# Due times shifted by phase in an attention and gated-mix kernel

## The chip, the cores and the metric

One core of a Trainium2 chip runs the whole program. The metric is the device time of one execution in microseconds (us). The kernel before was timed in three runs; the median is 744.59 us (743.41 to 746.06).

## The reference

The inputs are q, k and v of 8 batches, 8 heads, 576 positions and 64 elements, a scalar tau, and the weights of a gated mix. All is float32.

```python
def _attn_ref(q, k, v, tau):
    scores = scale * np.matmul(q, k.transpose(0, 1, 3, 2))
    thresh = np.max(scores, axis=-1, keepdims=True) - tau
    scores = np.where(scores >= thresh, scores, -1000000000.0)
    scores = scores - np.max(scores, axis=-1, keepdims=True)
    attn = np.exp(scores)
    attn = attn / (np.sum(attn, axis=-1, keepdims=True) + 1e-09)
    return np.matmul(attn, v)

def _moe_ref(x, w_val, conv_w, w_out):      # x: heads side by side, 8 x 576 x 512
    xp = np.concatenate([np.zeros((B, K - 1, D)), x], axis=1)
    for k in range(K):                      # K = 5 taps
        gate_pre += conv_w[k] * xp[:, k:k + S, :]
    gate = 1.0 / (1.0 + np.exp(-gate_pre))
    return gate * (x @ w_val) @ w_out
```

The threshold lies tau below the largest score of a row, so the maximum is taken first, and the exponentials under the threshold are dropped.

## The kernel before

A *job* is a pair of heads of one batch; there are 32 jobs, four to a batch. Each job has nine *score tiles*: one of 64 query rows of both heads together ("both"), and eight of 128 query rows of one head, so 288 tiles in all, numbered k in program order. A tile goes through these steps, each one a planned operation:

- `Tile.multiply` (L519, matmul at L537) on TensorE: scores into one of two PSUM rooms `s`. Keys are split into a high and a low float32r part, so an ordinary tile takes four matmuls and a tile of both heads six.
- `largest` (L541) on VectorE takes the row maximum; `weigh` (L547) on ScalarE makes `e`, the exponentials, and the threshold; `keep` (L560, L570) on VectorE drops what lies under the threshold, sums the rows, writes `pp` (or `pl` for both heads) and gives the room `s` back.
- `Group.divided` (L585, L603 on GpSimd, or L599 when ScalarE is free first) divides by the sums. The first batch divides later, after the product with v.
- `Group.turn` (L647, L659) on TensorE transposes blocks of three 128-column pieces into one of two PSUM rooms `tp`; `copy` (L663, L670) on ScalarE moves them into `T`.
- `Half.attended` (L722) has two parts for each half of the queries of a job: `attend` (L733), 20 matmuls of T and v into one of two PSUM rooms `acc`, and `evacuate` (L744; L742 on VectorE in the first batch), which copies into `xT`.

Around them run `Job.prepare` (L329: loads, splits and scaling of the next job's q and k; `place` at L368 lays blocks of q on GpSimd) and `subtract` (L295, L302: the low parts of splits, on GpSimd, for k, q, x and the gated values). `convolve` (L812) makes the high part of x (`xh`, L818 on ScalarE), the first tap (`tap0`, L828 on GpSimd), four more taps (L835 on VectorE) and the gate (L843). In the first batch the taps are matmuls (L788).

`products` (L864) runs once a batch: 96 matmuls of w_val with x, in chains of 12 into one `acc` each, gated on VectorE (L909), split into gh (`high`, L925 on ScalarE) and gl (`subtract`); then 96 of w_out (L882), evacuated on ScalarE (L947) and stored. Products come strictly one after another. Six rooms each hold xh and xl, so the first products of a batch must be done before the third job of the next can store its parts.

In what order all this stands on each engine's queue is settled when the program is built. Every operation has a *due* rank, in units of tiles, and a planned cost. `carry_out` (L134) walks through planned time. On each engine it finds the earliest time at which some operation can begin, given its inputs, its rooms and the engine; among all that can begin by then it takes the smallest due. The engines work through the resulting queues in order, waiting on semaphores. Due decides only between operations that are ready together in the plan.

Ranks that bear on the change: scores k - 8, with k the tile's number; reduce and weigh k - 8; keep k - 8; a division k - 4; a turn k - 3 + 0.1 c0; attend k - 2; evacuation of xT k - 4 (k being the last tile of the group or half). Products have the tile count at the batch's end plus 4, and 0.17 more for each matmul. xh, tap0 and the taps stand near the tile count at the job's end.

Of the kernel before, what the change touches and what calls it, by code (L numbers as in the profile page):

```python
# [20 lines left out]
AHEAD = False  # L21
TH = "ACT"
DIVIDE = ("ACT",)
DUE = (8, 8, 8)
PACE_M = 0.17
EARLY = 3
LATE = 1
ON_PE = (0, 1, 2, 3)
WARM = 10
FILL = 6  # L30


@with_exitstack
def tile_thresholded_attention_gated_mix(
# [88 lines left out]
    def op(engine, due, cost, done, emit, after=(), takes=(), gives=(), other=()):  # L123

        ways = {w[0]: w[1:] for w in ((engine, cost, done, emit), *other)}
        o = Op(ways, due, after, takes, gives)
        if not o.waits:
            for e in ways:  # L130
                open_ops[e].append(o)
        return o
# [41 lines left out]
    r_acc = Rooms(None, 0, None, None, None)  # L174
# [30 lines left out]
    def keep_busy(n):  # L205
        for _ in range(n):
            nc.tensor.matmul(r_tp.free[0][1], some[:, 0:P], some, start=True, stop=True)  # L207
# [21 lines left out]
    def from_f64(words, a, m, f, due, wide, after=(), takes=()):  # L229


        i32 = lambda t: t.bitcast(I32)
        hi, lo = lambda: words()[..., 1], lambda: words().bitcast(U16)[..., 1]
        least = 2.0**-15 * 1.125
        c1, c2 = (0.21, 0.345) if wide else (0.1, 0.12)
        square = op(
            "ACT", due, 0.34, 0.5, lambda: nc.scalar.square(f, hi().bitcast(F32)), after
        )
        last = op("DVEp", due, c1, c1 + 0.1, lambda: nc.vector.tensor_scalar(
            i32(m), hi(), 3, 0x3FFFFFFF, op0=ALU.logical_shift_left, op1=ALU.bitwise_and), after)  # L240
        last = op("DVEp", due, c2, c2 + 0.1, lambda: nc.vector.scalar_tensor_tensor(
            i32(a()), hi(), -(1 << 30), i32(m), op0=ALU.bitwise_and, op1=ALU.bitwise_or),
            [last], takes)
        last = op("DVEp", due, c2, c2 + 0.1, lambda: nc.vector.scalar_tensor_tensor(  # L244
            a(), f.bitcast(F32), least * least, a(), op0=ALU.is_ge, op1=ALU.mult), [last, square])
        last = op("DVEp", due, c1, c1 + 0.1, lambda: nc.vector.tensor_scalar(
            i32(m), i32(a()), -(1 << 23), None, op0=ALU.bitwise_and), [last])
        last = op("DVEp", due, c2, c2 + 0.1, lambda: nc.vector.scalar_tensor_tensor(
            f, lo(), 2.0**-36, m, op0=ALU.mult, op1=ALU.mult), [last])
        add = op("POOL", due, 0.71 if wide else 0.2, 0.8 if wide else 0.3,  # L250
                 lambda: nc.gpsimd.tensor_add(a(), a(), f.bitcast(F32)), [last])
        return last, add
# [218 lines left out]
    class Tile:  # L471
        def __init__(self, k, t, h, qc, grp):
# [16 lines left out]
            elif t.last == (h, qc):  # L489
                gives = [(r_Q, lambda: t.Q), (r_KH, lambda: t.KH), (r_KL, lambda: t.KL)]  # L490
            cost = 1.0 if t.i == 0 else 0.80 if both else 0.54
            self.scores = op(
                "PE", k - DUE[0], cost, cost + 0.26, self.multiply, after, [r_s], gives,
            )
            largest = op("DVE", k - DUE[1], 0.67, 0.84, self.largest, [self.scores], [r_nm])
            if TH == "ACT":
                after = [op("ACT", k - DUE[1], 0.83, 1.0, self.weigh, [largest], [r_e])]
            else:
                after = [
                    op("ACT", k - DUE[1], 0.64, 0.78, self.weigh, [largest], [r_e]),  # L500
                    op("DVE", k - 9, 0.13, 0.13, self.level, [largest]),
# [7 lines left out]
            else:  # L509
                room.append(r_sums)  # L510
            grp.kept = op(
                "DVE", k - DUE[2], 0.74, 0.96, self.keep, after, room,
                [(Scores(k), lambda: self.s), (r_e, lambda: self.e), (r_nm, lambda: self.nm)],
# [5 lines left out]
        def multiply(self):  # L519
# [18 lines left out]
            if self.k == EARLY - 1:  # L538
                keep_busy(FILL)

# [145 lines left out]
    class Half:  # L686
# [35 lines left out]
        def attended(self, k):  # L722
            t, j = self.t, self.j
            w, x0 = W[j], PAD + HALVES[j].start

            def attend():
                acc = self.acc = r_acc.take()
                T = self.T[:, :, 0:w]
                for c in (NKC, *range(NKC)):
                    for h, hs in enumerate(HEADS):  # L730
                        c0 = (2 * c + h) * D
                        chunk = 2 * NKC if c == NKC else h * NKC + c
                        nc.tensor.matmul(  # L733
                            acc[hs, :w], t.v[:, c0 : c0 + D], T[:, chunk, :],
                            start=c == NKC, stop=c == NKC - 1, skip_group_check=True,
                        )

            def evacuate():
                if j == 0:
                    t.xT = r_xT.take()  # L740
                if t.b < LATE:
                    nc.vector.tensor_mul(t.xT[:, x0 : x0 + w], self.acc[:, :w], self.R[:, W[0] - w :])  # L742
                else:
                    nc.scalar.copy(t.xT[:, x0 : x0 + w], self.acc[:, :w])  # L744

            cost = 5 * w / 600 + 0.1
            gives = [(r_T, lambda: self.T)]
            if j == 1:
                gives.append((r_v, lambda: t.v))
            made = op("PE", k - 2, cost, cost + 0.2, attend, [t.got_v, *self.copies], [r_acc], gives)  # L750
            cost = 0.31 if j == 0 else 0.255
            after = [made] if j == 0 else [made, t.got_x]
            gives = [(r_acc, lambda: self.acc)]
            if t.b < LATE:
                cost += 0.085
                after.append(self.inverses(k))
                gives.append((r_R, lambda: self.R))
            t.got_x = op("DVE" if t.b < LATE else "ACT", k - 4, cost, cost + 0.2, evacuate, after,
                         [r_xT] if j == 0 else [], gives)
            t.got_half.append(t.got_x)  # L760

# [311 lines left out]
```

## Time and profile before

| | |
|---|---|
| median of three runs | 744.59 us |
| profiled execution, its own time | 745.84 us |
| its span, first to last instruction | 744.1 us |
| TensorE busy | 728.5 us, 98% |
| ScalarE busy | 632.6 us, 85% |
| VectorE busy | 602.1 us, 81% |
| GpSimd busy | 525.7 us, 71% |
| mean granted TensorE clock | 0.997 |

Engines are called PE (TensorE; PEld is its weight load), ACT (ScalarE), DVE (VectorE), POOL (GpSimd) and SP (the queue that issues DMAs). Busy time is the union of an engine's instructions. The ends of matmuls are modelled, so a stop of PE shorter than a matmul's own length may not be seen as idle time. A wait is put down to the instruction whose end released it; L570 is line 570 of the kernel. Names such as `s<-KH,Q` say which tile is written from which.

### The profile page before, as it was taken

How to read it: one execution, taken by the hardware profiler on the slowest of the kernel's cores; microseconds unless marked ns; L12 is line 12 of the kernel's file. 1: busy time of each engine (PE TensorE's matmuls, PEld its weight loads, DVE VectorE, ACT ScalarE, POOL GpSimd, SP SyncE). 2: the span in 40 equal slices, each digit the busy share in tenths (PEclk: the TensorE clock that was granted, in tenths of full speed). 3: DMA queues.
4: the chain of work that ended last, by engine and by line, in shares of the span. 5: the costliest groups of instructions: out<-in, count | busy, mean ns of one | idle time of the engine just before them, and what ended most of it. 6: DMA issues, size and time to landing. Idle time of an engine off the chain costs nothing.

```text
span 744.1 us, 16295 instructions
## 1 busy us (share of the span) xinstructions
PE 728.5 (98%) x5454; PEld 615.4 (83%) x5454; DVE 602.1 (81%) x1290; ACT 632.6 (85%) x1461; POOL 525.7 (71%) x873
## 2 busy tenths in 40 slices
PE   9989999999999999999999999999999999999997
PEld 5767778888788887988888888988888888898897
DVE  6899988988888888888788888788888977888730
ACT  6698889889888888898988998899999889988832
POOL 4877568788688676788677886777678776666431
PEclk9999999999999999999999999999999999999999
DMA  7765566355655554456554465555456456523001
GB/s 217 185 160 154 137 168 161 74 144 145 160 137 137 125 158 117 124 132 168 148 131 114 124 161 158 125 124 144 125 142 153 120 135 170 128 61 85 18 33 64
DMA packets 51587, 97.96 MB, mean 132 GB/s; under 512 B 9008, under 2 KB 9520, under 8 KB 51504
## 3 DMA queue, kind: packets, MB, share of 16 engines
q1 hardware_dynamic: 51264, 96.61, 50.4%
q8 instruction: 44, 0.72, 0.4%
q10 hardware_dynamic: 240, 0.31, 0.2%
q14 instruction: 39, 0.32, 0.1%
HBM read 34.62 MB, written 9.44 MB: 59 GB/s over the span
## 4 chain that ended last, share of the span: by engine, by line
PE 83%; DVE 7%; ACT 7%; issue 1%; POOL 1%; POOLq 0%; ACTq 0%; DVEq 0%
PE acc L882 23%; PE acc L733 21%; PE s L537 21%; PE tp L659 16%; DVE pp L570 2%; ACT e L549 2%; DVE nm L543 2%; ACT T L670 2%; PE acc L788 1%; DVE pre L835 1%; ACT nm L551 1%; ACT xh L818 1%; PE tp L207 1%; DVE spare L244 1%; POOL gl L302 0%
## 5 line engine op out<-in xcount | busy, mean ns | idle before, releaser
L543 DVE TENSOR_REDUCE nm<-s 128x1 f32<-128x576 f32 x288 | 215.5, 753 | 49.3 <-PE s L537 47.0
L549 ACT ACTIVATE e<-s,nm 128x576 f32<-128x576 f32 x288 | 216.4, 751 | 23.1 <-DVE nm L543 13.3
L570 DVE SCALAR_TENSOR_TENSOR pp<-s,nm,e 128x576 f32<-128x576 f32 x256 | 207.3, 812 | 35.2 <-ACT nm L551 33.1
L670 ACT COPY T<-tp 128x384 f32<-128x384 f32 x384 | 176.1, 489 | 20.9 <-PE tp L659 19.4
L659 PE MATMUL tp<-ident,pp 128*128 128x128 f32 x1152 | 177.1, 274 | 2.3 <-ACT T L670 1.9
L733 PE MATMUL acc<-T,v 128*64 128x256 f32 (+1 forms) x1280 | 169.9, 412 | 0.7 <-ACT T L670 0.5
L537 PE MATMUL s<-KH,Q 128*128 128x288 f32 x496 | 154.9, 328 | 4.8 <-DVE pp L570 4.3
L603 POOL TENSOR_SCALAR pp<-pp,sums 128x576 f32<-128x576 f32 x151 | 126.7, 845 | 34.0 <-DVE sums L592 19.3
L659 PEld LDWEIGHTS tp<-ident,pp 128*128 128x128 f32 x1152 | 137.5, 140 | 9.7 <-issue 3.2
L537 PE MATMUL s<-KL,Q 128*128 128x288 f32 x496 | 138.9, 295 | 0.0
L733 PEld LDWEIGHTS acc<-T,v 128*64 128x64 f32 x1280 | 86.7, 137 | 62.1 <-issue 5.7
L537 PEld LDWEIGHTS s<-KH,Q 128*128 128x128 f32 x496 | 94.4, 190 | 28.0 <-DVE pp L570 10.3
L835 DVE SCALAR_TENSOR_TENSOR pre<-xT,cw,pre 128x576 f32<-128x576 f32 x112 | 105.8, 945 | 9.0 <-POOL pre L828 8.8
L537 PEld LDWEIGHTS s<-KL,Q 128*128 128x128 f32 x496 | 94.0, 190 | 0.3
L551 ACT ACTIVATE nm<-nm,less 128x1 f32<-128x1 f32 x288 | 85.6, 297 | 0.0
L590 POOL TENSOR_SCALAR sums<-sums 128x2 f32<-128x2 f32 (+1 forms) x144 | 42.3, 294 | 55.5 <-DVE pp L570 40.1
L882 PE MATMUL acc<-gl,woh 128*128 128x320 f32 (+1 forms) x256 | 78.4, 306 | 1.2 <-POOL gl L302 1.2
L882 PE MATMUL acc<-gh,woh 128*128 128x320 f32 (+1 forms) x256 | 78.6, 307 | 0.3 <-ACT xT L744 0.3
L882 PE MATMUL acc<-xh,wvh 128*128 128x320 f32 (+1 forms) x256 | 78.4, 306 | 0.0
L882 PE MATMUL acc<-xl,wvh 128*128 128x320 f32 (+1 forms) x256 | 78.3, 306 | 0.0
L882 PE MATMUL acc<-gh,wol 128*128 128x320 f32 (+1 forms) x256 | 78.1, 305 | 0.0
L882 PE MATMUL acc<-xh,wvl 128*128 128x320 f32 (+1 forms) x256 | 78.0, 305 | 0.0
(96 smaller groups left out, 1263.5 us busy)
## 6 DMA issues: line engine op xcount, KB each, us to landing
KH<-kh SPq DMA_DIRECT2D x124, 144.0 KB, 2.5
KL<-kl SPq DMA_DIRECT2D x124, 144.0 KB, 3.5
v<-vs SPq DMA_DIRECT2D x32, 320.0 KB, 3.1
k_r<-kT SPq DMA_DIRECT2D x31, 320.0 KB, 3.8
q_r<-qT SPq DMA_DIRECT2D x31, 288.0 KB, 3.5
outT<-o SPq DMA_DIRECT2D x31, 288.0 KB, 2.2
Q<-qh SPq DMA_DIRECT2D x62, 128.0 KB, 2.2
Q<-ql SPq DMA_DIRECT2D x62, 128.0 KB, 2.4
```

The costliest lines, as they stand in the source:

```text
L537: nc.tensor.matmul(s[:, a, :HS], w, m, start=i == 0, stop=i == len(terms) - 1)
L543: nc.vector.tensor_reduce(self.nm[:, 0:1], self.s[:, :, :HS], axis=AX.XY, op=ALU.max, negate=True)
L549: nc.scalar.activation(self.e, self.s[:, :, :HS], AF.Exp, bias=self.nm[:, 0:1])
L551: nc.scalar.activation(self.nm[:, 1:2], self.nm[:, 0:1], AF.Identity, bias=less, scale=-1.0)
L570: nc.vector.scalar_tensor_tensor(grp.p[:, i * S : (i + 1) * S].rearrange("p (a f) -> p a f", a=2), self.s[:, :, :HS], self.nm[:, 1:2], self.e,
L590: add = op("POOL", k - 4, 0.2, 0.33, lambda: nc.gpsimd.tensor_scalar(sums(), sums(), 1.0, 1e-9, op0=ALU.mult, op1=ALU.add), [self.kept])
L603: nc.gpsimd.tensor_scalar(v, v, ri(i), 0.0, op0=ALU.mult, op1=ALU.add)
L659: nc.tensor.transpose(tp[:, i * P : (i + 1) * P], self.p[:, k0 : k0 + P], ident)
L670: nc.scalar.copy(T[:, c0 : c0 + n, self.off : self.off + P], tp[:, 0 : n * P].rearrange("p (c q) -> p c q", q=P),)
L733: nc.tensor.matmul(acc[hs, :w], t.v[:, c0 : c0 + D], T[:, chunk, :], start=c == NKC, stop=c == NKC - 1, skip_group_check=True,)
L835: nc.vector.scalar_tensor_tensor(cv, t.xT[:, i : i + S], cw[:, g, i : i + 1], cv, op0=ALU.mult, op1=ALU.add)
L882: nc.tensor.matmul(taken[name, e, j][:, :w], wt[:, c, c0 : c0 + P], moving(c, i)[:, hs], start=n == 0, stop=n == NM - 1,)
```

## The change

A table gives shifts of due for thirteen kinds of operation, found by the name of the function that emits them and their first engine. Each has three numbers: for a due under 22, from 22 to under 50, and from 50 on. Besides, the ranks of reduce and weigh go from k - 8 to k - 8.5, and those of attend and of the xT evacuation are later by 1 for a job's first half and by 0.5 for its second. Nothing that is computed changes, nor any room or transfer.

```diff
--- before.py
+++ after.py
@@ -21,13 +21,29 @@
 AHEAD = False
 TH = "ACT"
 DIVIDE = ("ACT",)
-DUE = (8, 8, 8)
+DUE = (8, 8.5, 8)
 PACE_M = 0.17
 EARLY = 3
 LATE = 1
 ON_PE = (0, 1, 2, 3)
 WARM = 10
 FILL = 6
+SHIFT = {
+    ("Tile.multiply", "PE"): (0, 0, -8),
+    ("Tile.keep", "DVE"): (0, 0, -1),
+    ("Group.divided.<locals>.divide.<locals>.run", "POOL"): (0, -2, 0),
+    ("Group.turn.<locals>.run", "PE"): (-0.25, 0, -1),
+    ("Half.attended.<locals>.attend", "PE"): (0, 1, 0),
+    ("Job.prepare.<locals>.place.<locals>.run", "POOL"): (0, -2, 0),
+    ("subtract.<locals>.run", "POOL"): (0, 0, -0.5),
+    ("convolve.<locals>.high", "ACT"): (0, -2, 0),
+    ("convolve.<locals>.tap0", "POOL"): (0, 0, -2.5),
+    ("convolve.<locals>.gate", "ACT"): (0, 0, -1),
+    ("products.<locals>.product.<locals>.run", "PE"): (0, -4, 0),
+    ("products.<locals>.high", "ACT"): (0, 0.25, -4),
+    ("products.<locals>.evacuate.<locals>.run", "ACT"): (0, 0, -2),
+}
+PHASES = (22, 50)
 
 
 @with_exitstack
@@ -124,6 +140,9 @@
 
 
 
+        shift = SHIFT.get((emit.__qualname__.split("<locals>.", 1)[1], engine))
+        if shift:
+            due += shift[sum(due >= p for p in PHASES)]
         ways = {w[0]: w[1:] for w in ((engine, cost, done, emit), *other)}
         o = Op(ways, due, after, takes, gives)
         if not o.waits:
@@ -747,7 +766,7 @@
             gives = [(r_T, lambda: self.T)]
             if j == 1:
                 gives.append((r_v, lambda: t.v))
-            made = op("PE", k - 2, cost, cost + 0.2, attend, [t.got_v, *self.copies], [r_acc], gives)
+            made = op("PE", k - (1, 1.5)[j], cost, cost + 0.2, attend, [t.got_v, *self.copies], [r_acc], gives)
             cost = 0.31 if j == 0 else 0.255
             after = [made] if j == 0 else [made, t.got_x]
             gives = [(r_acc, lambda: self.acc)]
@@ -755,7 +774,7 @@
                 cost += 0.085
                 after.append(self.inverses(k))
                 gives.append((r_R, lambda: self.R))
-            t.got_x = op("DVE" if t.b < LATE else "ACT", k - 4, cost, cost + 0.2, evacuate, after,
+            t.got_x = op("DVE" if t.b < LATE else "ACT", k - (3, 3.5)[j], cost, cost + 0.2, evacuate, after,
                          [r_xT] if j == 0 else [], gives)
             t.got_half.append(t.got_x)
```

## Rows read from the trace of the kernel before

**Rows 1.** The page: busy us of each engine, share of span, instructions.

```profile
PE 728.5 (98%) x5454; PEld 615.4 (83%) x5454; DVE 602.1 (81%) x1290; ACT 632.6 (85%) x1461; POOL 525.7 (71%) x873
```

**Rows 2.** Groups by line on PE, 0 to 145 us: count | busy, mean | idle before.

```profile
L537 PE MATMUL s<-KH,Q 128*128 128x288 f32 x86 | 28.2, 344 | 2.9 <-DVE pp L570 2.9
...
L537 PE MATMUL s<-kh,bdq 128*128 128x288 f32 x24 | 5.5, 318 | 1.6 <-DVE pp L570 1.6
```

**Rows 3.** Stretches: length, busy PE, PEld, DVE, ACT, POOL, then clock, DMA, GB/s.

```profile
0.00:72.00 72.00, 67.90 (x408) 48.12 (x409) 59.88 (x140) 56.28 (x136) 49.48 (x109) 1.00 0.67 176
72.00:145.00 73.00, 69.89 (x496) 57.91 (x495) 66.43 (x155) 63.12 (x150) 51.11 (x85) 0.98 0.56 145
145.00:712.00 567.00, 563.08 (x4346) 482.36 (x4345) 468.12 (x985) 504.96 (x1160) 416.00 (x669) 1.00 0.51 129
712.00:744.10 32.10, 27.61 (x209) 27.03 (x208) 7.68 (x12) 8.24 (x17) 9.07 (x11) 0.99 0.13 47
```

**Rows 4.** Waits (us, times, longest): the first of 0 to 145, others of 145 to 712.

```profile
PE s L537 <- DVE pp L570: 4.7, 6, 1.8
...
PE s L537 <- DVE pp L570: 1.4, 5, 0.3
PE acc L882 <- ACT xT L744: 0.3, 1, 0.3
...
PEld s L537 <- DVE pp L570: 5.9, 16, 0.6
PEld s L537 <- DVE pre L835: 3.9, 8, 0.5
```

**Rows 5.** Timeline, 98 to 102 us, PE and ACT: start, length, what [idle before].

```profile
101.18 0.40 PE L537 MATMUL s<-KH,Q 128*128 128x288 f32 x1 [1.84 <-DVE pp L570]
...
98.68 0.78 ACT L599 ACTIVATE pp<-pp,sums 128x576 f32<-128x576 f32 x1
```

**Rows 6.** One stretch behind that wait; the clock is the third number from the end.

```profile
102.00:106.00 4.00, 4.00 (x23) 3.09 (x24) 3.19 (x8) 2.67 (x7) 1.51 (x5) 0.57 0.22 68
```

**Rows 7.** Taps: chain near 610 us; group of 145 to 712; line L835; POOL's timeline.

```profile
610.70 1.26 DVE pre L835
...
L835 DVE SCALAR_TENSOR_TENSOR pre<-xT,cw,pre 128x576 f32<-128x576 f32 x104 | 98.4, 946 | 0.6 <-POOL pre L828 0.4
...
L835 DVE SCALAR_TENSOR_TENSOR pre<-xT,cw,pre x112: 790/812/1459, 137.6 to 717.2; 128x576 f32<-128x576 f32 x112
...
609.79 1.56 POOL L302 TENSOR_TENSOR xl<-xT,xh 128x288 fp32r<-128x288 f32 x2 [0.26 <-ACT xh L818]
```

**Rows 8.** The chain near 545 us: start, length, what.

```profile
544.57 0.67 ACT xh L818
```

**Rows 9.** Groups by line on PE from 0 to 302.5 us.

```profile
L733 PE MATMUL acc<-T,v 128*64 128x320 f32 (+1 forms) x500 | 67.0, 414 | 0.7 <-ACT T L670 0.5 <-DVE g L909 0.3
L537 PE MATMUL s<-KH,Q 128*128 128x288 f32 x200 | 63.4, 333 | 3.6 <-DVE pp L570 3.4
...
L537 PE MATMUL s<-kh,bdq 128*128 128x288 f32 x52 | 11.4, 308 | 1.6 <-DVE pp L570 1.6
```

**Rows 10.** The chain near 699 us, pieces of score, products and turn.

```profile
698.48 0.53 PE s L537 x4
699.01 0.88 PE acc L882 x6
699.89 0.33 PE tp L659 x3
```

**Rows 11.** Waits of DVE and ACT for PE, 145 to 712 us.

```profile
DVE nm L543 <- PE s L537: 41.8, 81, 1.7
...
ACT xT L744 <- PE acc L733: 16.7, 25, 2.7
```

**Rows 12.** DMA issues: out<-in, count, KB each, us to landing.

```profile
KL<-kl SPq DMA_DIRECT2D x124, 144.0 KB, 3.5
```

**Rows 13.** Timeline of PE in the tail.

```profile
729.52 0.41 PE L882 MATMUL acc<-gl,woh 128*128 128x320 f32 x1 [1.21 <-POOL gl L302]
```

## The prediction

> **What bounds the kernel now.** I began with the page's busy line: TensorE (PE) has 98% of the span, ACT 85%, VectorE (DVE) 81%, GpSimd (POOL) 71% [rows 1]. A reorder takes no work away, so it can give back only time in which PE stands, and that is little: 744.1 - 728.5 = 15.6 us.
>
> The next view, stretches of the span, says where. I cut it where the change's phases turn. A score has due time T - 8 for tile number T, so phase 2 (due from 50) begins near tile 58. Counting the score products begun before 145 us (nine tiles of the first job, then two KH products for an ordinary tile and four kh products for a tile of both heads) gives 9 + 86/2 + 24/4 = 58 tiles [rows 2]. The same count puts the start of phase 1 (due 22, tile 30) near 72 us. PE stands 4.1 us in phase 0, 3.1 in phase 1, 3.9 in the 567 us of phase 2 and 4.5 in the tail after 712 [rows 3]. Phase 2 is PE-bound to 99.3%.
>
> Third, who made PE wait. Up to 145 us, 4.7 us in six waits are scores waiting for `keep` (L570), which frees their PSUM room; in phase 2 that is 1.4 us [rows 4]. Waits of the weight loads show more, since loads run ahead of PE: in phase 2, 16 loads of scores waited for `pp` and 8 for `pre`, 9.8 us in all or 0.41 each [rows 4]. Some of that is covered by the product still running, so PE's own loss in phase 2 lies between the 3.9 us seen and some 10; I take 6.
>
> Fourth, three of these waits from close by. The largest ends at 101.2: PE idle 1.84 us for `pp`, while ACT ran a division of 0.78 among other things ahead of the score's `e` [rows 5]. Behind it the granted clock falls to a mean of 0.57 for 4 us, most of it at 1.2 GHz [rows 6]; work worth 4 x 0.43 = 1.7 us is lost. So this one wait cost 1.84 + 1.7 = 3.5 us. In phase 2 there are two patterns. Near 610 a convolution tap (`pre`, L835) of 1.26 us sits ahead of the `keep` that the score needs [rows 7]; near 545 ACT's run of evacuation, copies and the cast `xh` (0.67) comes ahead of `e` [rows 8].
>
> **The change, part by part.** Every instruction stays; only ranks move. The list scheduler takes on each engine, among operations that can begin at the same planned time, the smallest due. So a shift acts only where two are ready at once.
>
> *Scores, -8 in phase 2.* Against products I expect little: both then wait mostly for rooms, and a score with a room already tends to lead. Against turns (-1 in phase 2) and attends it acts: at 302.5 us 9 + 200/2 + 52/4 = 122 score tiles had begun and 500/20 = 25 attends [rows 9]. The 26th attend is of tile k = 116, so its rank k - 2 = 114 stood level with the next score's 122 - 8. With the change it is 114.5 against 106. A turn block is 0.33 us, a score block 0.53, six products 0.88 [rows 10]. A score that overtakes a turn comes 0.33 earlier, the turn 0.53 later. What feeds on it: DVE waited 41.8 us for scores in phase 2 [rows 11], which shrinks, but DVE is not the bound. PE does the same work, so the direct gain is nothing. The price is cover: the turn that stood between `keep` and its score is gone, and PE works in order. Four more waits at 0.41, half hidden, are +0.8; the bounds are 0 (PE loses nothing) and +9.8 (all 24 waits doubled, none hidden). I take a value near the low end because now 24 of the 288 - 58 = 230 scores of phase 2 wait so.
>
> *In phase 2: keep -1, gate -1, gated splits -4 on ACT and all POOL subtractions -0.5, wo evacuation -2, tap0 -2.5; throughout, reduce and weigh -0.5 (DUE 8.5).* A `keep` that is ready now goes ahead of a tap or a gated product more often, and the xT evacuation, later by 1 or 0.5, leaves ACT to `e`. That bears on both patterns. But near 610 the tap had begun before `keep` was ready, and there no rank helps. I count one third of phase 2's 6 us as gained: -2.0. Bounds: 0, if every wait is of the not-ready kind, and -6. The gated splits, the gate and wo's evacuation are at nothing: the products' backlog covers them; without it their cost is a stop like the tail's, 1.21 us [rows 13], once a batch.
>
> *xT evacuation and attend later (k - 3 and k - 1 for the first half, k - 3.5 and k - 1.5 for the second), attend a further +1 in phase 1.* An attend behind products holds its T room longer, and the copies of T behind it on ACT wait; the evacuation holds one of two accumulators. At nothing: ACT waited 16.7 us for attends in phase 2 [rows 11], so the evacuation follows at once whatever its rank. If that cover fails, the price is a product held by an accumulator, 0.3 us, seen once [rows 4].
>
> *Phase 1: products -4, divisions, blocks of q (`place`) and the cast xh -2.* Products of the first batch with due under 50 (59 of 192) outrank scores by about one here. The large wait at 99 us lies in this stretch. Divisions pulled ahead on POOL leave ACT free of some; the same rank lets ACT take them ahead of `e` too. So that wait may go or stay. I count half of what is removable, the 3.1 us of idle and the 1.7 of clock: -2.4; bounds -4.8 and +3.5 (a second wait like it).
>
> *Phase 0: turn -0.25, reduce and weigh -0.5.* The waits there are 4.7 - 1.84 = 2.9 us, behind ACT and DVE work on weights whose ranks stay; -0.3, bounds 0 and -2.9.
>
> *Queues.* SP gets no shift of its own. What moves with the shifted steps: the copies of KH, KL and Q wait for rooms that a job's last score gives back, stores wait for wo's evacuation, q's copies for `place`. The slowest of the copies land in 3.5 us [rows 12]; two rooms of 9 tiles each (9 x 567/230 = 22 us) hide them, and without that cover a score would wait up to 3.5. *Tail.* After 712 PE has the last batch alone; its 1.21 us stop is for the last split `gl` [rows 13], with no competitor to outrank. At nothing.
>
> *Sum:* -0.3 - 2.4 - 2.0 + 0.8 = -3.9. The profiled execution took 745.84 (span 744.1 and 1.7 around it), so 741.9 by its measure; it stands 1.25 above the median of 744.59, and by the median the forecast is 740.7.
>
> *A rule against it.* The row first: the 104 taps of phase 2 have a mean of 946 ns, where the median of all is 812 and the longest 1459, some 14 us of DVE time lost; the piece of 1.26 us near 610 ran beside POOL's split of xl [rows 7]. The Trainium skill, "SBUF — State Buffer", section "Who interferes with whom", says that a VectorE instruction with two SBUF inputs and a GpSimd instruction that reads SBUF shut each other out, the later one being held for the whole of the first. By that rule tap0 2.5 earlier and splits 0.5 earlier could bring more taps under a split, and the sum would be that of rival 3 below; the trace agrees that taps are held, and does not show that they would be held more often.
>
> **Rivals.**
> 1. *Waits move, none is lost* (0.23). Plan and chip drift apart, and a new order finds other collisions. For it: the patterns near 610 and 545 are of work not ready, not of rank. That the change hardly does what it says, because few operations are ready together, ends here too. Against: the wait at 99 us is 3.5 us by itself, in a stretch that is reordered. Time 744.
> 2. *Scores without cover* (0.12). Scores that overtake turns reach PE just as `keep` ends, and every lateness of DVE or ACT halts PE. Place: phase 2. Price: 0.41 a wait, half hidden. With 24 more waits, that is +4.9, against the gain of phases 0 and 1 (-2.7): 746.8. It decides from about that doubling on, if phase 2 gains nothing itself. Against: PE has 99.3% there now.
> 3. *POOL under the taps* (0.05). If the 14 us that the taps lose double, the 3.9 us of loads that waited for `pre` [rows 4] double too: 740.7 + 3.9 = 744.6 with the other gains, 748.5 without them.
> 4. *All waits of phases 1 and 2 go* (0.12): 4.8 + 3.9 = 8.7, so 735.9.
>
> **How the numbers follow.** The forecast, 740.7, has 0.48; the rivals 0.23, 0.12, 0.05 and 0.12. A measurement of this kernel can tell some 0.3% (2.2 us) from no change. Faster: 0.48 + 0.12 = 0.60. Same: 0.23. Slower: 0.12 + 0.05 = 0.17. The range goes from rival 4 (736) to rival 2 (747).
>
> **What would show it.** Right: PE idle from 72 to 145 us falls from 3.1 to under 2 and no stretch there has half the clock; PE idle from 145 to 712 is under 3; DVE's wait for scores in phase 2 is clearly below 41.8; the tail's stop stays. Wrong: more than 24 loads of scores waiting for `pp` or `pre`, a mean of the taps above 946, a new idle stretch of 1.8 us with a clock fall behind it. The forecast fails if the order of phase 1 keeps its halt, or if the attention part runs so far ahead that `xh` has no free room and the products must catch up.

## The result and the profile after

The changed kernel took a median of 735.69 us against 743.26 for the kernel before on the same chip. The ratio is 0.9886, 95% interval 0.9873 to 0.9899: 8.5 us faster (the two medians lie 7.6 us apart). The forecast was 740.7, faster by 3.9, and the range ended at 736. The direction was right; the forecast gain is about half of the measured one, and the time lies just outside the range.

First the page of the changed kernel, its busy times, then its stretches (length; busy PE, PEld, DVE, ACT, POOL; clock, DMA, GB/s), and the last of these stretches in the kernel before. Lines of the changed kernel are 19 higher, so `keep` is L589, the score L556, a turn L678 and a tap L854.

```profile
PE 722.7 (98%) x5454; PEld 614.4 (84%) x5454; DVE 599.6 (82%) x1290; ACT 621.9 (85%) x1447; POOL 531.8 (72%) x887
```

```profile
0.00:72.00 72.00, 68.01 (x413) 48.73 (x414) 59.70 (x141) 56.05 (x136) 48.15 (x109) 1.00 0.66 175
72.00:145.00 73.00, 71.00 (x516) 58.88 (x516) 64.86 (x155) 64.84 (x157) 51.49 (x83) 1.00 0.62 156
...
145.00:700.00 555.00, 553.55 (x4304) 478.11 (x4302) 467.31 (x984) 492.68 (x1140) 423.11 (x686) 1.00 0.51 130
```

```profile
145.00:700.00 555.00, 551.08 (x4254) 473.15 (x4252) 463.99 (x976) 497.03 (x1141) 413.17 (x665) 1.00 0.51 131
```

The span went from 744.1 to 734.6, by 9.5 us. Against [rows 1, 3]: PE does the same 5454 instructions with 5.8 us less busy time and 3.7 less idle time. Phase 0 is nearly as it was (4.0 us idle, 4.1 before; 413 instructions for 408). Phase 1 has 2.0 us idle instead of 3.1, 516 instructions for 496, and its clock is 1.00 instead of 0.98 (0.02 x 73 = 1.5 us). From 145 to 700 us PE issues 4304 instructions; the kernel before issues 4254 in the same 555 us, with 551.08 busy. Fifty more are worth 50 x 555/4254 = 6.5 us. The mix of instructions in the stretch is not the reason: with each kind weighed by its usual time from start to start in the trace before, the work done there still rises by some 6 us. So phase 2 gave some 6.5 us, but only 553.55 - 551.08 = 2.5 of it were seen as idle time. The other 4.0 lie in time that counts as busy: 551.08/4254 = 129.5 ns an instruction before, 553.55/4304 = 128.6 after, with the clock at 1.00 in both. I take these for stops that the modelled ends of matmuls cover; the profile does not show them one by one.

Second the waits of the changed kernel (us, times, longest), 145 to 712 us, then the group of the taps there:

```profile
DVE nm L562 <- PE s L556: 37.0, 79, 1.8
...
PEld s L556 <- DVE pp L589: 5.6, 11, 1.3
PEld s L556 <- DVE pre L854: 2.5, 5, 0.5
```

```profile
L854 DVE SCALAR_TENSOR_TENSOR pre<-xT,cw,pre 128x576 f32<-128x576 f32 x108 | 99.6, 922 | 9.1 <-POOL pre L847 8.8
```

Against [rows 4, 7, 11]: 16 loads of scores wait for `pp` or `pre` instead of 24, 8.1 us in all instead of 9.8 (though the longest is now 1.3 instead of 0.6), DVE waits 37.0 us for scores instead of 41.8, and the taps' mean is 922 instead of 946. The taps take nearly as long as before; they less often stand in front of a score (5 loads wait for `pre` instead of 8).

The tail is unchanged, a stop of 1.20 against 1.21 [rows 13] (timeline of PE):

```profile
719.98 0.41 PE L901 MATMUL acc<-gl,woh 128*128 128x320 f32 x1 [1.20 <-POOL gl L321]
```

### The profile page after: what moved, and what is told of

Read it like the earlier page. It is cut to its first block, busy times and chain, and to the rows that moved or that the text cites. A ratio compares the mean times of both kernels' runs of the same rounds, so it can differ in the third digit from the quotient of the medians.

```text
span 734.6 us, 16310 instructions
## 1 busy us (share of the span) xinstructions
PE 722.7 (98%) x5454; PEld 614.4 (84%) x5454; DVE 599.6 (82%) x1290; ACT 621.9 (85%) x1447; POOL 531.8 (72%) x887
## 4 chain that ended last, share of the span: by engine, by line
PE 88%; ACT 3%; DMA 3%; DVE 2%; POOL 1%; issue 1%; SPq 1%; POOLq 0%; ACTq 0%
PE acc L901 26%; PE s L556 22%; PE acc L752 21%; PE tp L678 18%; DMA q_r<-qT 2%; PE acc L807 1%; ACT e L568 1%; DVE pp L589 1%; DVE nm L562 1%; DMA pre<-qT 1%; ACT T L689 1%; POOL gl L321 0%; ACT xh L837 0%; DMA Q<-ql 0%; DMA KL<-kl 0%
## 5 line engine op out<-in xcount | busy, mean ns | idle before, releaser
L589 DVE SCALAR_TENSOR_TENSOR pp<-s,nm,e 128x576 f32<-128x576 f32 x256 | 207.2, 813 | 33.5 <-ACT nm L570 29.6
L678 PE MATMUL tp<-ident,pp 128*128 128x128 f32 x1152 | 175.3, 273 | 1.1 <-ACT T L689 1.1
L622 POOL TENSOR_SCALAR pp<-pp,sums 128x576 f32<-128x576 f32 x165 | 138.4, 845 | 39.8 <-DVE sums L611 34.6
L556 PE MATMUL s<-KH,Q 128*128 128x288 f32 x496 | 152.2, 323 | 3.3 <-DVE pp L589 3.2
L678 PEld LDWEIGHTS tp<-ident,pp 128*128 128x128 f32 x1152 | 138.8, 140 | 7.2 <-ACT T L689 1.9
L556 PE MATMUL s<-KL,Q 128*128 128x288 f32 x496 | 138.2, 295 | 0.0
L556 PEld LDWEIGHTS s<-KH,Q 128*128 128x128 f32 x496 | 93.4, 188 | 29.1 <-issue 13.2
L854 DVE SCALAR_TENSOR_TENSOR pre<-xT,cw,pre 128x576 f32<-128x576 f32 x112 | 102.8, 918 | 9.1 <-POOL pre L847 8.8
L556 PEld LDWEIGHTS s<-KL,Q 128*128 128x128 f32 x496 | 93.6, 189 | 0.3
L609 POOL TENSOR_SCALAR sums<-sums 128x2 f32<-128x2 f32 (+1 forms) x144 | 40.3, 280 | 42.1 <-DVE pp L589 29.4
```

The lines of the kernel that those rows point to most:

```text
L556: nc.tensor.matmul(s[:, a, :HS], w, m, start=i == 0, stop=i == len(terms) - 1)
L589: nc.vector.scalar_tensor_tensor(grp.p[:, i * S : (i + 1) * S].rearrange("p (a f) -> p a f", a=2), self.s[:, :, :HS], self.nm[:, 1:2], self.e,
L609: add = op("POOL", k - 4, 0.2, 0.33, lambda: nc.gpsimd.tensor_scalar(sums(), sums(), 1.0, 1e-9, op0=ALU.mult, op1=ALU.add), [self.kept])
L622: nc.gpsimd.tensor_scalar(v, v, ri(i), 0.0, op0=ALU.mult, op1=ALU.add)
L678: nc.tensor.transpose(tp[:, i * P : (i + 1) * P], self.p[:, k0 : k0 + P], ident)
L854: nc.vector.scalar_tensor_tensor(cv, t.xT[:, i : i + S], cw[:, g, i : i + 1], cv, op0=ALU.mult, op1=ALU.add)
```

## Experiments

Below, "PE in 555 us" is the number of PE instructions between 145 and 700 us of a run's profile, with PE's idle time there, from one execution each (line numbers differ from run to run; the tiles' names tell which step it is); 43 instructions are 1%, some 5.6 us. It leaves out the start and phase 1, where single executions differ by themselves (last part of this document).

### The parts alone

Three parts were put alone into the kernel before, and the score's shift was taken out of the change.

```diff
--- p2_only: SHIFT with the third numbers only; DUE, attend, evacuation as before
--- p01_only: SHIFT with the first two numbers only; DUE, attend, evacuation as before
--- base_only: no SHIFT; DUE (8, 8.5, 8), attend and evacuation as changed
--- no_score: the change with
-    ("Tile.multiply", "PE"): (0, 0, -8),
```

> The kernel before with the third numbers of the shift table alone (due from 50 on); due 8, attend and evacuation as before. The trace of the changed kernel puts some 6 us of the 8.5 into the part from tile 58 on. If the ranks of phase 2 do it: 0.990 to 0.994 of before, and PE idle between 145 us and the last attend about 1.5 us instead of 3.9. If the gain needs the later attend and evacuation: 0.997 to 1.000.

> The kernel before with the first two numbers of the table alone (due under 50). If the wait near 99 us and the clock fall behind it go by these shifts: 0.995 to 0.997 (some 3 us), and no stretch at half the clock between 72 and 145 us. If that wait goes only with the reduce and weigh at 8.5 or with the attend: 0.999 to 1.001, and the half clock stays.

> The kernel before with no shift table, only reduce and weigh at k - 8.5 and attend and evacuation later by 1 and 0.5. My prediction put these at nothing to -1: 0.998 to 1.001. The rival that they carry the gain of phase 2, by leaving ACT to e after an attend: 0.992 to 0.995.

> The changed kernel without the score's -8 in phase 2, all else as changed. By my prediction the score's shift costs 0.8 us, so this would be 0.8 faster than the changed kernel: 0.987 of before. If the score's shift carries phase 2: 0.993 to 0.996, and the waits of weight loads for pp and pre are back near 24.

| kernel | ratio to before | 95% interval | PE in 555 us | idle, us |
|---|---|---|---|---|
| before | 1 | | 4254 | 3.92 |
| p2_only | 0.9984 | 0.9964 to 1.0003 | 4269 | 3.47 |
| p01_only | 1.005 | 1.0034 to 1.0066 | 4235 | 6.26 |
| base_only | 0.9975 | 0.9962 to 0.9989 | 4269 | 3.47 |
| no_score | 0.9926 | 0.9899 to 0.9952 | 4283 | 3.50 |
| the change | 0.9886 | 0.9873 to 0.9899 | 4304 | 1.45 |

The three parts alone sum to -0.2 + 0.5 - 0.25 = about 0; together they are -1.14%. So no part carries the gain, and a sum of parts, as I had made it, can't find it. p01_only does meet its condition in phase 1, where the clock stays at 1.00 and PE issues 502 instructions instead of 496; it loses in phase 0 (403 for 408) and above all behind 145 us (4235 for 4254). The score's shift, which I had put at a cost of 0.8 us, is worth 0.4% (3 us) where the rest of the change is present.

### Meaningless numbers on the ranks

If a sum of parts fails, the gain may lie in one order that the numbers happen to give. To test that, a fixed pseudo-random number between -0.25 and +0.25 tiles was added to each due (SEED is 1 or 2).

```diff
     def op(engine, due, cost, done, emit, after=(), takes=(), gives=(), other=()):
+        if engine != "SP":
+            count[0] += 1
+            due += 0.25 * ((count[0] * 7919 + SEED * 104729) % 1009 / 504.0 - 1.0)
```

> The kernel before, and to each due (SP's apart) a fixed pseudo-random number between -0.25 and +0.25 tiles is added, with no meaning. If the time follows the meaning of the ranks, a quarter of a tile changes little: 0.998 to 1.002. If it follows the accidents of the order (which operation happens to meet which), the time moves by as much as the single parts did, 0.3 to 0.7% either way, more likely up.

> The kernel before with the second set of meaningless numbers. It shows how far two sets lie apart with the old ranks: 0.997 to 1.004. If the kernel before were itself a lucky order, 1.004 or more.

> The changed kernel with the same meaningless numbers. If its gain comes from the meaning of its ranks: 0.987 to 0.991 of before. If the gain lies in one particular order that the numbers of the table happen to give together: most of it goes, 0.994 to 1.002.

> The changed kernel with a second set of meaningless numbers of the same size. Meaning: 0.987 to 0.991 again. Accident: 0.994 to 1.002, and not the time of the first set.

| kernel | ratio | 95% interval | PE in 555 us | idle, us |
|---|---|---|---|---|
| before + set 1 (jit_b1) | 1.0007 | 0.9994 to 1.002 | 4261 | 4.38 |
| before + set 2 (jit_b2) | 1.0015 | 1.0 to 1.003 | 4252 | 4.80 |
| change + set 1 (jit_a1) | 0.9952 | 0.9934 to 0.997 | 4296 | 2.28 |
| change + set 2 (jit_a2) | 0.9958 | 0.9944 to 0.9972 | 4295 | 1.95 |

Both theories are half right. Noise does little to the kernel before under either set, so there is no sign that it was a lucky order. It takes the change from 0.9886 to 0.9952 and 0.9958. About 0.45% (3.3 us) lasts against the kernel before, or 0.56% (4.2 us) against the kernel before with noise; the other 0.7% (some 5 us) belongs to the particular order. That rests on two sets. The third column says more: in phase 2 nearly all of the gain lasts (4296 and 4295, against 4304). Here is the stretch of jit_a1:

```profile
145.00:700.00 555.00, 552.72 (x4296) 477.07 (x4294) 468.09 (x986) 498.34 (x1152) 416.88 (x672) 1.00 0.50 131
```

Most of what noise takes away lies before 145 us (jit_a1 again):

```profile
0.00:72.00 72.00, 66.23 (x402) 46.84 (x402) 59.77 (x141) 55.87 (x135) 49.28 (x110) 1.00 0.68 175
```

It has 72.00 - 66.23 = 5.8 us of idle time in phase 0 instead of 4.0. Up to 145 us PE issues 928 instructions in the change, but 907 and 896 in jit_a1 and jit_a2; in the kernel before it issues 902, with noise 906 and 917. So the change's lead in phases 0 and 1 is of its particular order, and nothing of it lasts.

### The ranks of phase 2 together

```diff
--- base_p2: the change with every first and second number of SHIFT set to 0
--- jit_bp2: base_p2 with the first set of meaningless numbers
```

> The changed kernel without the first two numbers of the table: reduce and weigh at 8.5, attend and evacuation later, and the shifts of phase 2. If these parts work together and phases 0 and 1 only reach the stretch up to 145 us: 0.990 to 0.993, with PE idle after 145 us as in the changed kernel (1.5 us). If every part hangs on the whole order: 0.995 to 1.000, with PE idle after 145 us near 3.5.

> Reduce and weigh at 8.5, attend and evacuation later, the third numbers of the table, none of the first two, and the first set of meaningless numbers. Without that set this was 1.0013, with 565 us from tile 58 to the last attend. If all ranks that act in phase 2 together make the lasting gain and 1.0013 was an unlucky order: about 560 us there (559.3 and 560.5 with the whole change) and 0.994 to 0.997. If phases 0 and 1 set a state that phase 2 needs: 565 us or more and 0.999 to 1.003.

| kernel | ratio | 95% interval | PE in 555 us | idle, us |
|---|---|---|---|---|
| base_p2 | 1.0013 | 0.9994 to 1.0032 | 4254 | 5.97 |
| jit_bp2 | 0.9923 | 0.9903 to 0.9943 | 4298 | 1.28 |

Without noise the same ranks give nothing, with noise 0.8%. So 1.0013 was an unlucky order, and the shifts of phases 0 and 1 aren't needed for the gain of phase 2. With them, the same set gave 0.9952 (jit_a1). One piece of base_p2's bad luck is a PE stop of 1.36 us (timeline); its chain (start, length, what) shows how:

```profile
611.92 0.55 PE L673 MATMUL tp<-ident,pp 128*128 128x128 f32 x3 [1.36 <-POOL pp L617]
```

```profile
608.59 1.76 issue
610.35 0.02 POOLq L617
610.37 0.04 issue
610.40 0.74 POOL q_r L372
611.15 0.73 POOL pp L617
611.88 0.04 issue
611.92 0.55 PE tp L673 x3
```

And POOL's timeline, with the idle time before:

```profile
610.40 0.74 POOL L372 TENSOR_SCALAR q_r<-q_r,sc 128x576 f32<-128x576 f32 x1 [1.81 <-DMA q_r<-qT]
```

The division (`pp`) that PE's turn needs stands on POOL behind the scaling of the next job's q, and that waits for its load. My prediction had put the loads at nothing. Of the orders with all ranks of phase 2 and the products as in the change (the change, jit_a1, jit_a2, base_p2, jit_bp2) four have 4295 to 4304, one 4254.

### The score's shift, alone and left out, under noise

> The kernel before with the score's -8 in phase 2 and nothing else. My prediction: +0.8 us, 1.001. Backlog: scores that overtake turns carry the attention part a little ahead of the products, 0.995 to 0.998. Accident: 0.995 to 1.005.

> The kernel before with the score's -8 in phase 2 and the first set of meaningless numbers. If the score's rank carries the lasting part of the gain: 0.993 to 0.998, some 3 us under the same set without it (1.0007). If the gain of the score alone was accident too: 0.999 to 1.003.

> The same with the second set of meaningless numbers. Lasting: 0.993 to 0.998. Accident: 0.999 to 1.003.

> The changed kernel without the score's -8, with the first set of meaningless numbers. If the score's rank is all that lasts of the change and the rest is one lucky order: 0.998 to 1.003, that is 2 to 5 us above the same set with it (0.9952). If the other twelve shifts last too: 0.992 to 0.997.

> The changed kernel without the score's -8, with the second set of meaningless numbers. If the other ranks need the score's: above 565 us from tile 58 to the last attend and 1.002 to 1.009, as with the first set (570.7, 1.0079). If the first set was an unlucky order: 559 to 563 us, 0.993 to 0.998.

```diff
--- score_only: the kernel before with SHIFT of one entry; jit_s1, jit_s2: with sets 1 and 2
+    ("Tile.multiply", "PE"): (0, 0, -8),
--- jit_n1, jit_n2: no_score with sets 1 and 2
```

| kernel | ratio | 95% interval | PE in 555 us | idle, us |
|---|---|---|---|---|
| score_only | 0.9961 | 0.9946 to 0.9976 | 4286 | 1.72 |
| jit_s1 | 1.0015 | 1.0001 to 1.0029 | 4260 | 4.17 |
| jit_s2 | 1.0004 | 0.9992 to 1.0017 | 4254 | 3.92 |
| jit_n1 | 1.0079 | 1.0051 to 1.0107 | 4225 | 7.93 |
| jit_n2 | 1.0019 | 1.0006 to 1.0032 | 4263 | 4.98 |

Alone, the score's shift gains 0.4% and loses it under either set: an accident. Without it, the rest of the change loses its gain under either set as well: 1.0079 against 0.9952 with it, 1.0019 against 0.9958. So the lasting gain needs the score's -8 and its company; under noise neither has it alone. I had held the shift to cost 0.8 us, and it is worth 0.6% and 1.3% in company.

One thing that the shift does shows in the weight loads of turns. From 145 to 700 us these wait (summed over all releasers, "issue" left out) 5.7 us in the kernel before and 2.0 in score_only, 8.1 in no_score and 2.3 in the change. Under noise it is 5.6 and 7.6 in jit_b1 and jit_b2 against 4.1 and 3.0 in jit_s1 and jit_s2, and 11.4 and 5.3 in jit_n1 and jit_n2 against 2.5 and 0.4 in jit_a1 and jit_a2. In all six pairs the turns wait less once scores go ahead of them: the reading that fits is that a turn that comes later finds more of its inputs done. That alone is not the gain, since jit_s1 and jit_s2 have part of it and gain nothing. The largest of these waits in jit_n1 and in jit_a1 are:

```profile
PEld tp L682 <- POOL pp L626: 8.0, 8, 2.9
```

```profile
PEld tp L683 <- ACT T L694: 2.1, 3, 1.5
```

jit_n1 is no clean measure of that, though. It has a PE stop of 2.67 us at 201.7 and behind it a clock of 0.72 from 200 to 206 us (6 x 0.28 = 1.7 us lost). And its chain has the same pattern as base_p2's:

```profile
459.83 2.75 issue
462.58 0.02 POOLq L626
462.60 0.03 issue
462.63 0.75 POOL q_r L381
463.38 0.72 POOL pre L851
464.10 0.73 POOL pp L626
464.83 0.05 issue
464.87 0.88 PE tp L682 x6
```

Its waits, 145 to 700 us:

```profile
PE tp L682 <- POOL pp L626: 5.9, 3, 2.7
```

In all PE waits 5.9 us for three divisions; the one shown, a stop of 1.75 us, and the longest stand behind a q load. POOL waits 12.9 us for q's loads in that kernel's phase 2, 4.9 in the kernel before, 5.5 in the change and 4.1 in jit_n2. The difference of 0.6% between the second pair is the cleaner number.

### The products

A rival of mine, formed when the parts failed to add up, was the *backlog*: PE stands when the products have caught up with their inputs, so whatever keeps products behind the attention keeps PE filled.

```diff
--- prod_late: the kernel before with one entry
+    ("products.<locals>.product.<locals>.run", "PE"): (8, 8, 8),
--- prod_first: in the change, (0, -4, 0) becomes
+    ("products.<locals>.product.<locals>.run", "PE"): (0, -4, -8),
--- prod_late_a: in the change, (0, -4, 0) becomes
+    ("products.<locals>.product.<locals>.run", "PE"): (0, -4, 8),
```

> The kernel before with one edit: every product's due 8 tiles later, no other shift. Theory of the backlog: PE stands when the products have caught up with their inputs (at the joint of two batches and between w_val and w_out) and the order has nothing to fill with; products that rank last keep a store of work. Then from tile 58 to the last attend about 560 us instead of 565.8, ratio 0.991 to 0.995. Theory of the scores (they must come early, whatever the products do): no change, 0.998 to 1.002. Theory of accident: anything within 0.5%.

> The changed kernel with products 8 tiles earlier from due 50 on, so that they keep pace with the scores again. Backlog: it is spent, the stretch from tile 58 to the last attend goes back to 564 to 567 us and the ratio to 0.996 to 1.001; fewer than 20 products are left at the starts of batches. Scores or keep by themselves: still 0.988 to 0.992.

> The changed kernel with products another 8 tiles later from due 50 on. Backlog: the store is there already, so little more, 0.986 to 0.990; PE from tile 58 to the last attend 557 to 560 us. If a longer store blocks the rooms of xh and so the attends: 0.992 or above, with waits of ACT or PE for xh's rooms.

| kernel | ratio | 95% interval | PE in 555 us | idle, us |
|---|---|---|---|---|
| prod_late | 1.0024 | 1.0011 to 1.0037 | 4250 | 4.72 |
| prod_first | 1.033 | 1.0301 to 1.0358 | 4079 | 19.42 |
| prod_late_a | 0.9935 | 0.9913 to 0.9956 | 4263 | 4.07 |

prod_first keeps the products at their inputs. Counted as in [rows 2], when the first score of a batch begins, only 6 to 8 products of the batches up to the last but one are still owed, where the kernel before owes 14 to 47 and the change 31 to 56. It costs 3.3% over the kernel before and 4.5% over the change, more than I had expected. PE then has nothing else to do while it waits; first its stretch, then two of its waits:

```profile
145.00:700.00 555.00, 535.58 (x4079) 455.10 (x4079) 451.09 (x937) 478.72 (x1095) 398.19 (x653) 1.00 0.50 131
```

```profile
PE s L556 <- DVE pp L589: 11.4, 19, 1.0
...
PE tp L678 <- POOL xl L321: 3.6, 6, 0.6
```

So a spent backlog is dear; that half is shown. The other half isn't: prod_late leaves the backlog at the first batches as it was (19 and 14 owed), probably because products are already taken only when nothing else is ready, and prod_late_a has more owed in places (64) and is slower than the change. And jit_b1 owes 31 to 47, much like the change, with 4261 instructions in the stretch. So what the change gains isn't explained by backlog.

## Why the prediction was right or wrong

**What bounds the kernel: right; the limit drawn from it: not.** PE had 98% before and after. The 15.6 us of idle time were taken for all that a reorder can give back, but 5.8 of the 9.5 us came out of time that the page counts as busy, some 1.5 of it by the clock. The 15.6 were not reached, and they limit nothing.

**Scores, -8: wrong, and the step that failed is "the direct gain is nothing ... the price is cover".** I reasoned on one score and one turn. Over a whole order, the score's rank with the others of phase 2 makes a lasting gain: 4295 to 4304 PE instructions in 555 us in four orders of five, against 4225 and 4263 in the two noisy orders without it (4283 in no_score, without noise). The term was +0.8 us; in its company the runs put the shift at -3 us in the change's own order and at -4.5 or more under noise. The cover was not lost: loads of scores that wait for `pp` or `pre` fell from 24 to 16. And the turn's delay, which I had entered without any gain, spares waits of the turn's own loads, in all six pairs.

**Keep, reduce, splits and the others of phase 2, -2.0: sign right, mis-sized.** The term was a third of 6 us, with the scores -1.2 net; measured are some 6.5. The 6 itself was too small: I took what loads and PE showed as waits, while of the 6.5 us gained only 2.5 had been seen as idle time of PE. How much of it each of these ranks has, apart from the score's, was not tried.

**Phase 1, -2.4: the size came out, in good part by luck.** Idle time fell by 1.1 us and the clock gave 1.5, 2.6 together. The stop near 99 us is gone, but another came at 107.5 in its place, and no_score shows that it can be as dear as the old one (below). The clock's part needs no new rank: prod_late has the old stop without the fall and issues 508 instructions in phase 1, against 496 before and 516 in the change. And under noise the lead at 145 us is gone.

**Phase 0, -0.3, and the tail, nothing: right.** Phase 0 gave 0.1 us of idle time (by its five instructions more, at most 0.9 us), and the tail's stop is 1.20 against 1.21.

**The signs** said less than the time. Those for being right came, but for phase 1's idle time, which is 2.0 and not under 2; of those for being wrong none came in the change.

**Queues at nothing: wrong as a bound.** Loads of q did reach PE, through POOL, by 1.36 us at one place of base_p2 and by 1.75 and 2.67 in jit_n1. In the change they cost phase 1 a stop.

**The sum of terms: wrong as a method.** The parts measured alone give about 0, the whole -8.5 us. Rival 1, that a new order merely finds other collisions, is the nearest to what single parts do; it missed that all ranks of phase 2 together have a lasting effect. Rival 2 (scores without cover) didn't come, rival 3 (POOL under the taps) neither: 922 against 946. Taps are still held, with a mean of 922 ns over 108 of them where an undisturbed one took about 0.8 us. The Trainium skill, "SBUF — State Buffer", section "Who interferes with whom", has a VectorE instruction with two SBUF inputs and a GpSimd instruction that reads SBUF shut each other out; the trace agrees again that taps are held. Only, the order decides whether a held tap has a score behind it. Rival 4 (all waits of phases 1 and 2 go, 735.9) is the nearest in time, but not as told: 2.0 and 1.45 us of idle time are left, and most of what phase 2 gave had not been seen as waits of PE.

**What stays open:** which of the phase 2 ranks besides the score's are needed, and by what chain of work the two act together; the shorter waits of turns are one piece of it. The 5 us of the particular order are told apart from the lasting part by two sets of noise, not explained stop by stop.

## What to carry to other kernels

When an order comes out of a list scheduler, a change of ranks is two things, a rule and one particular order; noise on all ranks, some tenths of the unit, tells how much is which, and parts tried alone don't. Here four tenths to a half of the gain lasted. Let the work that everything waits for lead and the filler trail: the reverse (prod_first) was the one edit that cost several per cent, though making the filler trail further (prod_late, prod_late_a) gained nothing. Where an engine's ends are modelled, the idle time that a profile shows is no limit to what an order can give; count its instructions in a fixed stretch as well.

## What the runs showed of the hardware

The same order costs different amounts in different executions. On PE, the change and no_score have the same order up to 160 us. Near 105 us both wait for a load of q, through POOL, a weight split, ACT and `keep`. In the change the load ends at 104.0 (the first line, of the chain), POOL has waited 4.00 us by then and PE stands 0.60 (timeline), and the clock stays at 1.00 (stretches):

```profile
98.10 5.90 DMA q_r<-qT
```

```profile
104.16 0.75 POOL L377 TENSOR_SCALAR q_r<-q_r,sc 128x576 f32<-128x576 f32 x1 [4.00 <-DMA q_r<-qT]
...
108.17 0.40 PE L556 MATMUL s<-KH,Q 128*128 128x288 f32 x1 [0.60 <-DVE pp L589]
```

```profile
105.00:110.00 5.00, 4.22 (x26) 3.41 (x24) 2.79 (x9) 4.48 (x11) 4.08 (x7) 1.00 0.40 107
110.00:120.00 10.00, 10.00 (x78) 8.31 (x77) 9.57 (x26) 10.00 (x24) 6.90 (x11) 1.00 0.54 127
```

In no_score POOL's scaling of q begins 0.5 us later, after a wait of 5.14; PE stands 1.76 us and is then granted 0.83 of the clock over the next stretch (timeline, then stretches):

```profile
104.69 0.75 POOL L376 TENSOR_SCALAR q_r<-q_r,sc 128x576 f32<-128x576 f32 x1 [5.14 <-DMA q_r<-qT]
...
108.70 0.40 PE L555 MATMUL s<-KH,Q 128*128 128x288 f32 x1 [1.76 <-DVE pp L588]
```

```profile
105.00:110.00 5.00, 3.05 (x18) 2.30 (x16) 1.91 (x5) 3.45 (x9) 4.55 (x8) 1.00 0.30 79
110.00:120.00 10.00, 10.00 (x68) 8.78 (x67) 8.64 (x25) 8.81 (x21) 5.33 (x8) 0.83 0.46 111
```

The score comes 0.53 us later than in the change. (The stop is 1.16 longer because PE was 0.63 us ahead when it began to wait.) The clock then takes another 0.17 x 10 = 1.7 us. So half a microsecond at a load became more than two.

The length of the stop alone does not decide it. In [rows 5, 6] a stop of 1.84 us was followed by such a fall. prod_late has the order of the kernel before on PE, ACT, DVE and POOL up to 424 us, and the same stop, but its clock stays at 1.00 (timeline, then the stretch of [rows 6]):

```profile
101.35 0.40 PE L544 MATMUL s<-KH,Q 128*128 128x288 f32 x1 [1.84 <-DVE pp L577]
```

```profile
102.00:106.00 4.00, 4.00 (x35) 2.87 (x34) 4.00 (x11) 3.04 (x8) 1.68 (x5) 1.00 0.25 73
```

The timed executions fit this: of 20 executions of the kernel before, beside no_score, 8 had a mean granted clock of 1.000 and took 742.65 to 744.03 us, and 12 had 0.997 or 0.998 and took 744.15 to 746.30. Of no_score's four executions only the profiled one was below 1.000. So comparing orders by one stretch of one execution near such a stop tells more about the load and the clock than about the order.
